# A gated recurrence with a low-rank mixer on one Trainium2 core: rows packed in 96 partitions, logarithms of the first groups summed by matmul, and a new instruction order

## The chip, the cores and the metric

The kernel runs on one core of a Trainium2 chip. The metric is the device time of one execution in microseconds (us); the time before is the median of three runs. Profiles are of one execution each. Engines in the profile are PE (TensorE matmuls), PEld (TensorE weight loads), DVE (VectorE), ACT (ScalarE), POOL (GpSimd) and SP (SyncE, which here issues nearly all DMAs).

## What is computed

The inputs are float32: q, k, v, a_re, a_im of shape (4, 8, 768, 48), that is 4 batches, 8 heads, 768 steps, 48 features, and U (768 x 32), V (32 x 768), w_ch1 (384 x 1536), w_ch2 (1536 x 384). The first half is a recurrence with a complex decay per feature, the second a mixer:

```
mag = sqrt(a_re^2 + a_im^2);  scale = min(mag, 0.999) / (mag + 1e-6)
for t in range(768):                     # per batch and head
    S = (a[t] * scale[t])[:, None] * S + outer(k[t], v[t])     # complex S, 48 x 48
    y[t] = q[t] @ real(S)
x = y as (4, 768, 384)
u = x + (x^T @ U @ V)^T
out = u + relu(u @ w_ch1) @ w_ch2
```

## The kernel before, in words

**Chunks and groups.** The sequence is cut into 24 chunks of 128 steps (6 a batch). Two chunks make a group; groups are numbered 0 to 11. The decays turn into sums of logarithms of magnitudes and sums of angles along the chunk, so that the recurrence becomes matrix products inside a chunk plus a state G (features x 48 per head) carried from chunk to chunk.

**Per group** (`gates`, lines 617 to 821). `magnitudes_of` computes on ScalarE and VectorE two arrays per step and feature: `l`, the clamped half logarithm of the squared magnitude, and `y`, the logarithm of one plus 1e-6 over the magnitude. Their sum is the logarithm that is summed along time. In the kernel before, VectorE adds them in place (group 0: a tensor_scalar and an add, lines 658 and 660; later groups: a ScalarE Relu and a fused subtract-and-add, lines 662 and 663). `within` then sums along time with matmuls against constant 0/1 matrices: `es ps` and `ef ps`, 128 x 384 each, exponentials of which scale q and k; `of_blocks` sums over blocks into `tot`, whose exponential E goes by four DMAs on SP to the transposed array T. Groups 3 to 11 (`SPLIT`) split each float32 array into two rounded halves (GS) and use the faster fp32r matmul; groups 0 to 2 use plain float32 matmuls (lines 696 and 735). A float32 matmul shows as two records in the trace.

The angle is arctan on ScalarE, times a sign of a_re (n), shifted by a quarter turn. Groups 0 to 2 (`BITS`) take the sign on VectorE from the sign bit; groups 3 to 11 take it with a ScalarE Sign (line 681) and scale and shift with a ScalarE Identity (line 763). Groups 0 to 2 add the quarter turn with one more matmul (line 799). The phase sum `ph` follows by matmul, F is its fraction of a turn, and `cs` holds cosine and sine.

**Per chunk.** `prep` multiplies q and k by es and by cs into QKC (per head a row of cosine part and a row of sine part, each 48 long in a space of 64), and transposes it on TensorE (line 860): 112 rows, of which 48 to 63 are a gap of zeros. `chain` builds products of blocks (inner, corners), scales by T on VectorE, and computes the state update dk (line 996, tile columns 0 to 63 and 64 to 111) and the output y.

**The mixer** (`mixer`) runs per two chunks once a batch is through: rank, mixed, uTp, up, down, and from m = 7 on products with fewer multiplications (few).

**The order.** Nothing is scheduled at run time. Every operation has a number in one common order of all engines, written out in `ORDER`; each engine's instructions stand in the order of these numbers. `SPARE` says before which operation how many units of filler are to be issued: matmuls of the 128 x 128 identity into a free PSUM tile (`idle`, lines 1507 to 1520), at most three units to a matmul, a unit being 128 columns. Where no PSUM tile is free, none is issued. The kernel before asks for 153 units; its program holds 91, of which 8 stand before the first es ps, 9 between it and the first ef ps. Filler waits for nothing but its PSUM tile, and later matmuls stand behind it.

Of the kernel before, what the change touches and what calls it, by code (L numbers as in the profile page):

```python
# [39 lines left out]
        ("POOL", "load"): {0: [14], 1: [34], 1.5: [84], 2: [31]},  # L40
        ("DVE", "load"): {1: [58]},
# [6 lines left out]
        ("ACT", "gates"): {0: [1, 2, 4, 6, 7, 16, 17, 22, 23, 29, 28, 45, 70, 71], 1: [24, 27, 38, 39, 41, 42, 46, 47, 65, 64, 67, 68], 2: [129, 108,  # L48
# [10 lines left out]
        ("DVE", "gates"): {0: [5, 8, 13, 18, 19, 54, 49], 1: [30, 21, 40, 43, 44, 51, 50], 2: [111, 143, 156, 185, 169], 4: [277, 322, 323, 372, 356],  # L59
# [109 lines left out]
        ("POOL", "small"): {0: [932, 933], 1: [1119, 1116, 1117], 2: [1337, 1278, 1338], 3: [1670, 1446, 1515], 4: [1778, 1776, 1777], 5: [2049, 1855,  # L169
        2008], 6: [2154, 2101, 2162], 7: [2343, 2276, 2342], 8: [2633, 2632, 2648], 9: [2629, 2634, 2663], 10: [2635, 2627, 2636]},  # L170
        ("POOL", "angles"): {6: [615], 8: [708, 733], 10: [882, 931], 12: [1097], 14: [1273, 1302], 16: [1472, 1516], 18: [1669], 20: [1879, 1913],
        22: [2039, 2077]},
        ("DVE", "mixing"): {7: [2018, 2019, 2021, 2030, 2032, 2024, 2040, 2102, 2108, 2115, 2120, 2125, 2027]},
}

# [1413 lines left out]
```

## Time and profile before

| quantity | value |
|---|---|
| runs | 626.64, 626.9, 627.37 us; median 626.9 |
| span of the profiled execution | 627.0 us; 0.1 above the median |
| busy time: PE, PEld | 609.9, 526.2 us |
| busy time: DVE, ACT, POOL | 499.7, 415.8, 38.1 us |
| PE busy in filler (line 1519) | 30.6 us |
| first es ps, first inner, first rank matmul begin | 8.79, 31.28, 116.27 us |

The span runs from the first to the last instruction of the execution. Matmuls are pipelined, so a record's duration is longer than the distance from one start to the next; distances between starts tell what a matmul costs TensorE. In a line of a timeline stand start, duration, engine, line of the kernel, operation, output and inputs, shapes, count, and in brackets the idle time of the engine before it with what ended it.

### The profile page before, as it was taken

What the parts mean: (1) busy time and instruction counts of PE and PEld (TensorE: products, weight loads), DVE (VectorE), ACT (ScalarE), POOL (GpSimd) and SP (SyncE); (2) the same over time, 40 slices, a digit from 0 to 9 for tenths busy, and PEclk for the clock granted to TensorE, in tenths of its full rate; (3) what the DMA queues carried; (4) which work ended last, traced back from release to release, by engine and by line L of the source; (5) the groups of instructions that cost most, each with busy time, mean ns of one, the idle gap of its engine ahead of it and who ended that gap; (6) DMA issues with size and microseconds to landing.
All of it is one profiled execution on the core that took longest, in us unless ns stands there. A gap on an engine that the chain in (4) does not pass through costs nothing.

```text
span 627.0 us, 23447 instructions
## 1 busy us (share of the span) xinstructions
PE 609.9 (97%) x10380; PEld 526.2 (84%) x10380; DVE 499.7 (80%) x887; ACT 415.8 (66%) x807; POOL 38.1 (6%) x79
## 2 busy tenths in 40 slices
PE   6998989999999999999999999999999999999998
PEld 3566767666889889889989989888999998999997
DVE  6899999888999979758977867788989884464554
ACT  6999999999898988687787867688433431202010
POOL 5000000000001010010000100000100100000100
PEclk7999999999999999999999999999999999999999
DMA  8864565644143252541512512601203020000101
GB/s 211 191 146 115 135 136 132 155 111 104 33 80 76 50 120 44 99 89 28 99 37 46 113 40 46 124 19 25 63 21 60 9 51 3 1 1 1 45 14 44
DMA packets 173685, 45.74 MB, mean 73 GB/s; under 512 B 167632, under 2 KB 170384, under 8 KB 173584
## 3 DMA queue, kind: packets, MB, share of 16 engines
q1 hardware_dynamic: 171376, 39.90, 30.1%
q0 software_dynamic: 2208, 4.35, 2.1%
q8 instruction: 81, 1.33, 0.9%
q14 instruction: 20, 0.16, 0.1%
HBM read 33.59 MB, written 4.72 MB: 61 GB/s over the span
## 4 chain that ended last, share of the span: by engine, by line
PE 77%; ACT 4%; DVE 3%; DMA 1%; issue 1%; SPq 0%; ACTq 0%; DVEq 0%
PE down L1356 24%; PE up L1122 15%; PE few L1222 11%; PE dk L996 3%; PE tr L860 3%; PE y L1035 3%; PE inner L910 2%; PE down L1313 2%; PE inner L907 2%; PE tot L741 2%; PE y L1027 2%; PE mixed L1089 2%; PE es ps L692 1%; PE ef ps L692 1%; PE uTp L1107 1%; PE corners L971 1%
## 5 line engine op out<-in xcount | busy, mean ns | idle before, releaser
L1122 PE MATMUL up<-uT,w 128*128 128x256 f32 x504 | 116.9, 383 | 0.0
L387 DVE TENSOR_TENSOR QK<-QK,T 112x512 f32<-112x512 f32 (+2 forms) x144 | 102.1, 732 | 8.4 <-PE inner L910 4.3
L1122 PEld LDWEIGHTS up<-uT,w 128*128 128x128 f32 x504 | 93.6, 190 | 12.5
L1356 PE MATMUL down<-w,h 128*128 128x192 f32 x396 | 72.2, 331 | 0.0
L384 ACT ACTIVATE gate<-gate 128x768 f32<-128x768 f32 (+1 forms) x82 | 64.8, 795 | 7.4 <-DVE GS L791 3.2
L1356 PEld LDWEIGHTS down<-w,h 128*128 128x128 f32 x396 | 64.1, 190 | 1.5 <-issue 0.7
L871 ACT COPY QK<-tr 112x512 f32<-112x512 f32 x96 | 51.2, 590 | 14.6 <-PE tr L860 14.3
L390 DVE TENSOR_TENSOR xo<-down,xo 128x192 f32<-128x192 f32 (+1 forms) x79 | 29.9, 387 | 27.5 <-PE down L1356 27.0
L387 DVE TENSOR_TENSOR QKC<-qk,cs 128x768 f32<-128x768 f32 x44 | 41.7, 955 | 6.3 <-ACT cs L384 3.6
L1230 ACT COPY h<-few 128x512 f32<-128x512 f32 x30 | 17.2, 586 | 40.8 <-PE few L1222 40.8
L1356 PE MATMUL down<-stage 128*128 128x192 f32 x198 | 37.6, 331 | 0.0
L1111 ACT COPY uT<-uTp 128x384 f32<-128x384 f32 x22 | 10.0, 479 | 41.4 <-PE uTp L1107 26.9
L1222 PE MATMUL few<-gate,w 128*128 128x128 f32 x280 | 34.8, 275 | 0.0
L1298 POOL DMA_DIRECT2D out_dram<-xo x32 | 19.2, 644 | 243.3 <-DVE xo L390 140.0
L860 PEld LDWEIGHTS tr<-ident,QKC 64*112 64x112 f32 x768 | 24.5, 130 | 10.7 <-issue 4.7
L1222 PEld LDWEIGHTS few<-gate,w 128*128 128x128 f32 x280 | 33.3, 192 | 0.0
L1356 PEld LDWEIGHTS down<-stage 128*128 128x128 f32 x198 | 32.1, 190 | 0.7 <-issue 0.2
L779 POOL DMA_DIRECT2D gate<-F x15 | 12.0, 799 | 327.9 <-DVE w L578 113.5
L860 PE MATMUL tr<-ident,QKC 64*112 64x64 f32 x768 | 29.4, 221 | 2.3 <-DVE QKC L387 1.6
L381 ACT ACT_TABLE_LOAD x24 | 30.8, 1283 | 1.1 <-PEq L1573 0.7
L384 ACT ACTIVATE h<-up 128x512 f32<-128x512 f32 x42 | 24.6, 596 | 9.8 <-PE up L1122 9.5
L976 ACT COPY AT<-corners 32x128 f32<-32x128 f32 x96 | 24.2, 255 | 9.6 <-PE corners L971 8.3
(200 smaller groups left out, 1285.4 us busy)
## 6 DMA issues: line engine op xcount, KB each, us to landing
stage<-in_moe_w_ch_dram SPq DMA_DIRECT2D x12, 768.0 KB, 5.0
qk<-in_q_dram SPq DMA_DIRECT2D x24, 192.0 KB, 3.2
qk<-in_k_dram SPq DMA_DIRECT2D x24, 192.0 KB, 2.7
VP<-in_v_dram SPq DMA_DIRECT2D x24, 192.0 KB, 3.6
gate<-in_a_re_dram SPq DMA_DIRECT2D x22, 192.0 KB, 3.4
gate<-in_a_im_dram SPq DMA_DIRECT2D x22, 192.0 KB, 3.4
AT<-DG SPq DMA_DIRECT2D x96, 32.0 KB, 2.3
T<-E SPq DMA_DIRECT2D x48, 48.0 KB, 2.9
```

Source lines behind the costliest of these rows:

```text
L381: ACT(1.37, rank, lambda: nc.scalar.preload_act_table_set(name), writes=[TABLE])
L384: return nc.scalar.activation(out=o, in_=i, func=f, **kw)
L387: nc.vector.tensor_tensor(out=o, in0=a, in1=b, op=OP.mult)
L390: nc.vector.tensor_tensor(out=o, in0=a, in1=b, op=OP.add)
L860: nc.tensor.transpose(out=get(*ps[r])[0:DQ, h], in_=get(*qkc)[at, h].rearrange("p u d -> p (u d)")[:, 0:DQ], identity=ident[at, at], tile_ ...
L871: nc.scalar.copy(out=to, in_=a)
L976: ACT(0.36, RR, lambda r=r, u=u: nc.scalar.copy(out=get(*ATi).rearrange("p (a u) t -> p a u t", u=2)[r:r + BLK, :, u, BLK:2 * BLK], in_=ge ...
L996: nc.tensor.matmul(out=get(*dk[r])[x:end, h], lhsT=get(*ks)[at, h, x // DP, 0:end - x], rhs=get(*VPi)[at, h], start=True, stop=True, tile_ ...
L1122: nc.tensor.matmul(out=get(*ps)[:, e], lhsT=w1[:, f, (ff + e) * 128:(ff + e + 1) * 128], rhs=get(*uT)[:, f], start=(f == 0), stop=(f == KD ...
L1222: nc.tensor.matmul(out=get(*ps)[:, q], lhsT=w()[:, q * 128:(q + 1) * 128], rhs=v[0](), start=(n == 0 and q == 0), stop=True, skip_group_ch ...
L1298: queue.dma_start(out=out[b, c * CH:(c + 1) * CH, lo:hi], in_=get("xo", i)[:, lo:hi])
L1356: nc.tensor.matmul(out=get(*to)[:, part], lhsT=x(j), rhs=y[:, j], start=(first and j == 0), stop=(j == KH - 1), skip_group_check=not first)
```

## The change

Four things are done to the arithmetic and one to the order:

1. The rows of QKC and T lie without a gap: 96 rows (cosine 0 to 47, sine 48 to 95) in place of 112. The memsets of the gap go. The transposes have 96 columns of weights in place of 112, the second tile of dk 32 in place of 48, and the VectorE and ScalarE operations on QK, T, G and GM 96 partitions in place of 112.
2. In groups 0 to 2, `y` and `l` are not added on VectorE; es ps, ef ps and tot are each accumulated by two matmuls, one on y and one on l. Groups 1 and 2 lose the ScalarE Relu for a VectorE tensor_scalar, as group 0 had it.
3. All groups take the sign from the sign bit on VectorE.
4. In groups 3 to 11 the quarter turn is added in the copy that splits z in two halves, and in the difference after it; the ScalarE Identity goes.
5. `ORDER` and `SPARE` are replaced as a whole. The new `SPARE` asks for 154 units, and the program holds all: 60 before the first es ps (20 matmuls of 384 columns in a row), then 13, 6, 20, 10, 6, 3, 7 and 4 up to the transposes of the second chunk, 25 later. On SP, the four loads of group 0's gates and the small constants go ahead of the first load of w_ch1. On TensorE, es ps and ef ps of both first chunks follow one another directly, then both tot.

The diff without `ORDER`:

```diff
-SPARE = {20: 8, 32: 9, 62: 1, 66: 1, 73: 1, 82: 5, 91: 1, 113: 6, 116: 1, 119: 8, 140: 8, 153: 6, 157: 4, 167: 1, 168: 1, 207: 6, 216: 1, 217: 1, 282:
-         1, 352: 2, 436: 1, 514: 5, 518: 5, 527: 4, 546: 4, 547: 25, 551: 12, 596: 2, 601: 1, 606: 3, 624: 1, 632: 3, 646: 1, 653: 1, 664: 1, 672: 2,
-         678: 5, 694: 1, 695: 1, 717: 1, 718: 2}
+SPARE = {23: 60, 83: 13, 90: 6, 106: 20, 127: 10, 129: 6, 131: 3, 139: 7, 144: 4, 258: 12, 442: 2, 481: 4, 608: 3, 617: 4}
...
+    DQ = 2 * D
     DP = 64
-    DQ = DP + D
...
-        QKC.append(singles.tile([128, H, 2, DP], FP, name="QKC%d" % n))
-        nc.gpsimd.memset(QKC[n][:, :, :, D:DP], 0.0)
+        QKC.append(singles.tile([128, H, 2, D], FP, name="QKC%d" % n))
...
-        nc.gpsimd.memset(TS[n], 1.0)
...
-            if on_dve:
+            if g not in SPLIT:
                 DVE(c_one(W), R1, lambda: nc.vector.tensor_scalar(out=t(l), in0=t(l), scalar1=-0.5, scalar2=-LNMAX, op0=OP.mult,
                                                                   op1=OP.max), [], [L])
-                DVE(cd, R1, lambda: add(t(l), t(l), t(y)), Y, [L])
...
-            if g in BITS:
-                DVE(c_one(W), R1, lambda: nc.vector.tensor_scalar(out=t(n).bitcast(U32), in0=t(ar).bitcast(U32), scalar1=0x80000000,
-                                                                  scalar2=INV_PI, op0=OP.bitwise_and, op1=OP.bitwise_or), AR, [N])
-            else:
-                ACT(ca + 0.09, R1, lambda: act(t(n), t(ar), AF.Sign, bias=tiny), AR, [N])
+            DVE(c_one(W), R1, lambda: nc.vector.tensor_scalar(out=t(n).bitcast(U32), in0=t(ar).bitcast(U32), scalar1=0x80000000,
+                                                              scalar2=INV_PI, op0=OP.bitwise_and, op1=OP.bitwise_or), AR, [N])
...
-                    PE(0.65, R1, lambda: nc.tensor.matmul(out=get(*to), lhsT=m.bitcast(FP), rhs=of(l, i), start=True, stop=True),
-                       [L, name], [to, ("sums", g, i)], takes=[keeps], steps=2)
+                    def two():
+                        for u, a in enumerate((y, l)):
+                            nc.tensor.matmul(out=get(*to), lhsT=m.bitcast(FP), rhs=of(a, i), start=(u == 0), stop=(u == 1))
+                    PE(1.3, R1, two, [L, y + (i,), name], [to, ("sums", g, i)], takes=[keeps], steps=4)
...
-                        nc.tensor.matmul(out=get(*ps)[u * 64:u * 64 + w, p], lhsT=get(*l)[:, h:h + w], rhs=total, start=True,
-                                         stop=True, tile_position=(0, u * 64))
+                        for n, a in enumerate((y, l)):
+                            nc.tensor.matmul(out=get(*ps)[u * 64:u * 64 + w, p], lhsT=get(*a)[:, h:h + w], rhs=total, start=(n == 0),
+                                             stop=(n == 1), tile_position=(0, u * 64))
...
-            if g not in BITS:
-                ACT(ca + 0.09, R2, lambda: act(t(z), t(z), AF.Identity, scale=1.0 / math.pi, bias=fourth), [], Z)
...
-                    ACT(c_act(DM), R2, lambda: nc.scalar.copy(out=of(a, i), in_=of(z, i)), [zi], [a + (i,)])
+                    ACT(c_act(DM) + 0.09, R2, lambda: act(of(a, i), of(z, i), AF.Identity, bias=fourth), [zi], [a + (i,)])
...
-                DVE(c_dve(DM), R2, lambda: nc.vector.tensor_tensor(out=of(b, i), in0=of(z, i), in1=of(a, i).bitcast(FP), op=OP.subtract),
-                    [zi, a + (i,)], [b + (i,)])
+                DVE(c_dve(DM), R2, lambda: nc.vector.scalar_tensor_tensor(out=of(b, i), in0=of(z, i), scalar=0.25, in1=of(a, i).bitcast(FP),
+                                                                          op0=OP.add, op1=OP.subtract), [zi, a + (i,)], [b + (i,)])
...
-                        nc.tensor.transpose(out=get(*ps[r])[0:DQ, h], in_=get(*qkc)[at, h].rearrange("p u d -> p (u d)")[:, 0:DQ],
+                        nc.tensor.transpose(out=get(*ps[r])[0:DQ, h], in_=get(*qkc)[at, h].rearrange("p u d -> p (u d)"),
...
-                        nc.tensor.matmul(out=get(*dk[r])[x:end, h], lhsT=get(*ks)[at, h, x // DP, 0:end - x], rhs=get(*VPi)[at, h],
+                        nc.tensor.matmul(out=get(*dk[r])[x:end, h], lhsT=get(*ks)[at, h].rearrange("p u d -> p (u d)")[:, x:end], rhs=get(*VPi)[at, h],
```

More of the change, by code (lines that the diff above doesn't have):

```diff
@@ L30 @@
 ORDER = {
[9 rows of a table removed]
-        ("POOL", "load"): {0: [14], 1: [34], 1.5: [84], 2: [31]},
-        ("DVE", "load"): {1: [58]},
[6 rows of a table removed]
-        ("ACT", "gates"): {0: [1, 2, 4, 6, 7, 16, 17, 22, 23, 29, 28, 45, 70, 71], 1: [24, 27, 38, 39, 41, 42, 46, 47, 65, 64, 67, 68], 2: [129, 108,
[10 rows of a table removed]
-        ("DVE", "gates"): {0: [5, 8, 13, 18, 19, 54, 49], 1: [30, 21, 40, 43, 44, 51, 50], 2: [111, 143, 156, 185, 169], 4: [277, 322, 323, 372, 356],
[10 rows of a table removed]
-        ("ACT", "angles"): {0: [72, 86, 98, 100, 103], 1: [76, 106, 112, 114, 126], 2: [210, 231, 251, 240, 241, 242, 263, 269, 271], 4: [375, 395,
[5 rows of a table removed]
@@ L172 @@
-        22: [2039, 2077]},
-        ("DVE", "mixing"): {7: [2018, 2019, 2021, 2030, 2032, 2024, 2040, 2102, 2108, 2115, 2120, 2125, 2027]},
-}
-SPARE = {20: 8, 32: 9, 62: 1, 66: 1, 73: 1, 82: 5, 91: 1, 113: 6, 116: 1, 119: 8, 140: 8, 153: 6, 157: 4, 167: 1, 168: 1, 207: 6, 216: 1, 217: 1, 282:
-         1, 352: 2, 436: 1, 514: 5, 518: 5, 527: 4, 546: 4, 547: 25, 551: 12, 596: 2, 601: 1, 606: 3, 624: 1, 632: 3, 646: 1, 653: 1, 664: 1, 672: 2,
-         678: 5, 694: 1, 695: 1, 717: 1, 718: 2}
[9 rows of a table added]
+        ('POOL', 'load'): {0: [22], 1: [55], 1.5: [594], 2: [41]},
@@ new lines @@
+        ('DVE', 'load'): {1: [18]},
[6 rows of a table added]
+        ('ACT', 'gates'): {0: [0, 4, 2, 9, 14, 10, 16, 43, 51, 32, 36, 44, 61, 64], 1: [6, 12, 24, 29, 25, 31, 40, 45, 49, 47, 53, 59], 2: [122, 89,
[10 rows of a table added]
+        ('DVE', 'gates'): {0: [8, 27, 28, 15, 62, 58], 1: [13, 21, 30, 34, 50, 73], 2: [113, 155, 149, 192, 200], 4: [236, 310, 306, 327, 336], 6:
[10 rows of a table added]
+        ('ACT', 'angles'): {0: [68, 84, 95, 92, 101], 1: [71, 97, 105, 107, 116], 2: [197, 228, 247, 238, 240, 242, 266, 268, 286], 4: [374, 397, 415,
[5 rows of a table added]
+        ('DVE', 'angles'): {0: [77, 85], 1: [78, 98], 2: [210, 232, 248], 4: [378, 401, 416], 6: [577, 590, 592, 600, 614, 615, 630], 8: [688, 705,
[4 rows of a table added]
@@ new lines @@
+        ('DVE', 'prep'): {0: [93, 102, 104], 1: [119, 125, 137], 2: [204, 244, 251], 3: [277, 288, 295], 4: [390, 422, 433], 5: [392, 439, 471], 6:
[6 rows of a table added]
+        ('ACT', 'prep'): {0: [112, 108, 118, 120], 1: [145, 147, 151, 152], 2: [260, 259, 264, 263], 3: [308, 313, 339, 340], 4: [443, 441, 445, 444],
[4 rows of a table added]
+        ('DVE', 'rest'): {0: [117, 154, 159, 193, 142, 162, 183], 1: [178, 227, 231, 261, 213, 234, 237, 256], 2: [269, 315, 326, 357, 293, 323, 328,
[8 rows of a table added]
+        ('DVE', 'levels'): {0: [121, 134, 140, 132, 135, 143], 1: [168, 207, 212, 187, 201, 217], 2: [270, 281, 292, 279, 287, 311], 3: [352, 364,
[9 rows of a table added]
@@ new lines @@
+        ('ACT', 'levels'): {0: [138], 1: [208], 2: [300], 3: [391], 4: [470], 5: [519], 6: [751], 7: [837], 8: [946], 9: [1008], 10: [1156], 11:
[14 rows of a table added]
+        ('ACT', 'rest'): {0: [177, 186, 179, 171, 221, 215, 220], 1: [252, 254, 250, 253, 280, 282, 273], 2: [356, 355, 359, 353, 377, 379, 381], 3:
[10 rows of a table added]
+        ('ACT', 'small'): {0: [596, 290, 362, 504, 383, 483, 612, 566, 611, 628], 1: [726, 752, 803, 811, 777, 823, 858], 2: [958, 893, 1094, 1131,
[4 rows of a table added]
+        ('DVE', 'small'): {0: [276, 606, 618, 627, 636, 665, 673, 664, 645, 652, 732, 743], 1: [687, 734, 686, 821, 844, 854, 861, 872, 882, 904, 915,
[25 rows of a table added]
@@ new lines @@
+        ('POOL', 'small'): {0: [801, 750], 1: [1099, 947, 1069], 2: [1334, 1264, 1425], 3: [1614, 1507, 1535], 4: [1749, 1702, 1777], 5: [2031, 1930,
+        1953], 6: [2216, 2142, 2206], 7: [2377, 2223, 2364], 8: [2637, 2634, 2636], 9: [2524, 2541, 2618], 10: [2606, 2621, 2639]},
+        ('POOL', 'angles'): {6: [603], 8: [703, 736], 10: [878, 892], 12: [1080], 14: [1270, 1294], 16: [1457, 1479], 18: [1628], 20: [1840, 1884],
+        22: [2007, 2081]},
+        ('DVE', 'mixing'): {7: [1997, 2010, 2001, 2011, 2029, 2000, 2039, 2092, 2102, 2120, 2113, 2114, 2056]},
+}
@@ L301 @@
     PL = H * HC
-    BITS = range(SPLIT[0])
     PUT = (0, 2), (4, 6), (8, 10)
@@ L443, in w2_of @@
         return w2.rearrange("p (j x) m -> p j x m", x=2)[:, :, x, y * DH:(y + 1) * DH]
-    leps, lmax, tiny = column("leps", math.log(1e-6)), column("lmax", LNMAX), column("tiny", 1e-30)
+    leps, lmax = column("leps", math.log(1e-6)), column("lmax", LNMAX)
     magic, fourth, quarter = column("magic", MAGIC), column("fourth", 0.25), column("quarter", math.pi / 2)
@@ L744, in of_blocks @@
             else:
-                PE(0.51, R1, sums, [l, ("total", 0), ("sums", g)], [ps], way=1, takes=[e], steps=4 * HH)
+                PE(0.82, R1, sums, [l, y + (i,), ("total", 0), ("sums", g)], [ps], way=1, takes=[e], steps=8 * HH)
             used = 2 * D if g in SPLIT else 64 + D
@@ L988, in chain @@
         for r in parts_k:
-            psum(dk[r], "Y", [128, H, D], [128, H, DP])
+            psum(dk[r], "Y", [128, H, D], [128, H, HC])
         def state(h0):
```

23 lines of the change are left out of this document (6 added, 17 removed), and 248 rows, old and new, of the table ORDER.

## The prediction

> **What bounds the kernel now.** I read the page's busy shares first, then the table of busy times by stretch for TensorE alone, cut at the places that matter here, then the timeline of TensorE up to the first row sums.
>
> ```profile
> PE 609.9 (97%) x10380; PEld 526.2 (84%) x10380; DVE 499.7 (80%) x887; ACT 415.8 (66%) x807; POOL 38.1 (6%) x79
> ```
>
> TensorE is busy for 609.9 of 627.0 us, so its own timeline can be used as a ledger: the span is its work, plus its fillers (the matmuls of `ident` that `idle` issues), plus its waits.
>
> ```profile
> core 0: us, PE busy (x), PEclk, DMA share, GB/s
> 0.00:1.42 1.42, 0.00 (x0) 1.00 0.00 0
> 1.42:5.00 3.58, 3.58 (x6) 1.00 0.87 164
> 5.00:8.79 3.79, 0.01 (x1) 0.91 0.94 272
> 8.79:14.92 6.13, 6.12 (x10) 0.50 1.02 260
> 14.92:31.28 16.36, 14.82 (x167) 1.00 0.82 187
> 31.28:116.27 84.99, 79.36 (x2019) 1.00 0.58 135
> 116.27:157.00 40.73, 39.43 (x365) 1.00 0.49 117
> 157.00:600.00 443.00, 442.61 (x7664) 1.00 0.25 50
> 600.00:627.00 27.00, 23.97 (x169) 1.00 0.10 34
> ```
>
> The second column is the length of the stretch, the third TensorE's busy time. Its waits are 1.42 us before `ident` exists, 3.03 us at the end (the last sum and its store), and between them 3.79 + 1.54 + 5.63 + 1.30 + 0.39 = 12.65 us. All but 0.39 us of these lie before 157 us; from there to 600 us TensorE alone sets the pace, and nothing that VectorE or ScalarE saves there is worth time. Before that, another engine is full too:
>
> ```profile
> 48.00:64.00 16.00, 14.16 (x412) 10.81 (x411) 15.86 (x25) 15.36 (x32) 0.00 (x0) 1.00 0.47 107
> 64.00:80.00 16.00, 15.30 (x385) 11.29 (x384) 16.00 (x28) 15.79 (x31) 0.00 (x0) 1.00 0.59 142
> 80.00:96.00 16.00, 13.85 (x399) 10.39 (x398) 15.97 (x25) 15.75 (x32) 0.00 (x0) 1.00 0.57 136
> ```
>
> Here the columns are TensorE, its weight loads, VectorE, ScalarE and GpSimd. VectorE (15.97 of 16) and ScalarE are full, and TensorE waits for them. So a change decides the time in two ways: by what it adds to or takes from TensorE anywhere, and by when the chain of the first groups lets VectorE begin.
>
> **The fillers and the first matmuls.** This part weighs most, and it is in the new order, not in the arithmetic.
>
> ```profile
> 1.42 3.58 PE L1519 MATMUL tr<-ident 128*128 128x384 f32 x6 [1.42 <-POOL ident masks.py:199]
> 8.79 1.62 PE L696 MATMUL es ps<-GL,mid 128*128 128x384 f32 x2 [3.79 <-DVE GL L390]
> 10.21 4.05 PE L1519 MATMUL tr<-ident 128*128 128x384 f32 x6
> 13.42 0.56 DVE L390 TENSOR_TENSOR GL<-GL,gate 128x384 f32<-128x384 f32 x1
> 14.05 1.25 PE L696 MATMUL ef ps<-GL,fore 128*128 128x384 f32 x2
> 15.13 0.39 PE L1519 MATMUL tr<-ident 128*128 128x128 f32 x2
> 15.35 0.81 PE L696 MATMUL es ps<-GL,mid 128*128 128x384 f32 x2
> 16.00 0.81 PE L696 MATMUL ef ps<-GL,fore 128*128 128x384 f32 x2
> 16.64 0.39 PE L1519 MATMUL tr<-ident 128*128 128x128 f32 x2
> 17.69 1.09 PE L735 MATMUL tot<-total,GL 128*64 128x32 f32 x32 [0.66 <-ACT es L384]
> 21.59 0.91 PE L801 MATMUL ph<-gate,prefix 128*128 128x384 f32 x2
> 26.23 0.27 PE L860 MATMUL tr<-ident,QKC 64*112 64x64 f32 x1 [0.23 <-DVE QKC L387]
> 31.28 0.89 PE L910 MATMUL inner<-QK 112*32 112x48 f32 x64
> ```
>
> A float32 matmul leaves two records. Nine units of filler (one unit is 128 columns) run from 10.21 to 14.05: 0.427 us each. At full clock a matmul of 384 columns starts 0.65 us after the one before (15.35 to 16.00): 0.215 us a unit. The granted clock was 0.50 in 8.79:14.92 and 1.00 after it, so TensorE ran 6.13 us on end before it sped up, and the 3.58 us at the start, at the same slow pace, hadn't sufficed.
>
> The kernel before issues 91 units: 8, then 9 at the slow pace (3.58 + 3.84 = 7.4 us), then 74 spread out. The order of the changed program has 154: **60 in one block before the first es ps**, then 13, 6, 20, 10, 6, 3, 7, 4 up to the second chunk's transposes, and 25 later. They wait for nothing, and what stands behind them waits for all of them. I take the slow pace for 6.13 us again: 14.4 units by 7.55, the other 45.6 x 0.215 = 9.8, and the first es ps starts at 17.3 us where it started at 8.79. It is ready earlier: both chunks' logarithms were done at 13.98 (the row at 13.42), behind more loads than the new order puts ahead of them. The block costs 15.9 for 7.4: **+8.5 us**. Bounds: full clock from 5.00 on gives a start at 16.1 (-1.2), one more microsecond or two at half pace +1.3. The Trainium skill (TensorE: Matmul & The Clock Gate, section "What's actually happening") lets the clock rise after one busy window of about 3.4 us that runs freely; by 3.4 us the start would be near 15.8 and the sum 1.5 us less, and here the first stretch of 3.58 us speaks against the short end.
>
> ScalarE feels the block at once: in its new order the two exponentials of es stand ahead of the x logarithm and reciprocal of both chunks, so arctan, F, cs and QKC are queued behind the block. Following the new order of TensorE behind 17.3: eight matmuls 5.2, 32 tot 2.2, four ph and one carry 3.3, 55 units 11.8, 32 transposes 1.1, 16 dk 0.6: the first inner at 41.5, against 31.28. Waits cover none of it, for the other engines' steps are shorter than TensorE's: from the end of tot (18.78) to ph of z (21.59) they took 2.8, and TensorE now has two ph and 13 units there, 4.1; from there to the transposes (26.23) 4.6, against 7.5 now; from there to the inner 5.1, against 5.1. On SP both chunks' gates go ahead of the first weight load, and on GpSimd five memsets go; both only make operands earlier that the block then holds back.
>
> The other 94 units against 74: 20 x 0.215 = **+4.3 us**.
>
> **Logarithms summed on TensorE.** In the first three groups es ps, ef ps and tot take y and l one after the other. That is 12 matmuls of 384 columns more, 12 x 0.65 = 7.8, and 48 of tot at 1.09 / 16 = 0.068 each, 3.3. Against it, one es ps and one ef ps were at half pace (10.21 - 8.79 = 1.42, 15.13 - 14.05 = 1.08) and aren't any more: -1.2. **+9.9 us** (11.1 at 0.75 a matmul, as after a short tile).
>
> **Packing in 96.** No moving operand gets shorter; only weight loads do: the transposes' from 112 to 96 columns, the second tile of dk from 48 to 32.
>
> ```profile
> 66.03 1.16 PE L860 MATMUL tr<-ident,QKC 64*112 64x64 f32 x32
> 67.12 2.86 PE L1122 MATMUL up<-uT,w 128*128 128x256 f32 x12
> 43.17 1.12 PE L735 MATMUL tot<-total,w 128*64 128x32 f32 x32
> 44.22 1.56 PE L1519 MATMUL up<-ident 128*128 128x384 f32 x4
> 104.73 1.47 PE L741 MATMUL tot<-total,GL 128*96 128x32 f32 x16
> 106.03 0.60 PE L692 MATMUL ef ps<-GS,fore 128*128 128x384 f32 x2
> L860 PEld LDWEIGHTS tr<-ident,QKC 64*112 64x112 f32 x768 | 24.5, 130 | 10.7 <-issue 4.7
> ```
>
> Thirty-two transposes take 1.09 us, 68 ns a pair of halves. What a column of weights costs I estimate from tot: 96 columns 1.30 / 16 = 81 ns, 64 with 48 beside them 1.05 / 16 = 66 ns: 0.47 ns a column. 16 x 0.47 = 7.5 ns for each of 384 pairs: **-2.9 us**; bounds 0, if the load is hidden, and -5.8, if both of a pair count. In dk the tile beside stays at 64 columns: 0, at most -2.4. VectorE and ScalarE go by elements per partition, so 96 for 112 gives them nothing.
>
> **Signs, quarter turn, adds.**
>
> ```profile
> L384 ACT ACTIVATE gate<-gate,tiny 128x768 f32<-128x768 f32 x9 | 8.4, 938 | 0.0
> L384 ACT ACTIVATE gate<-gate,fourth 128x768 f32<-128x768 f32 x9 | 8.4, 931 | 2.3 <-DVE gate L760 2.1
> L384 ACT ACTIVATE GL<-GL,lmax 128x768 f32<-128x768 f32 x10 | 9.3, 930 | 0.1
> L578 DVE TENSOR_SCALAR w<-w 128x768 uint32<-128x768 uint32 x12 | 6.7, 562 | 0.0
> L390 DVE TENSOR_TENSOR GL<-GL,gate 128x384 f32<-128x384 f32 x2 | 1.1, 568 | 0.3 <-ACT gate L384 0.2
> ```
>
> ScalarE loses 9 signs, 9 quarter turns and one Relu in each of groups 1 and 2: 8.4 + 8.4 + 1.9 = 18.7 us. VectorE gains 9 x 0.56 = 5.0 and loses two adds (1.1) and about 0.4 in each of groups 1 and 2. Nearly all of it falls behind 100 us. I cost it at nothing: TensorE's work hides it, and if that cover were gone, the 5.0 would be the most it could cost. Before 116 us it helps only through waits, which come next.
>
> **Waits.** With TensorE later and fuller before 116 us, the 3.79 is filled, and much of 1.54 + 5.63 + 1.30 goes: VectorE's operations between the first inner and the rank matmuls stay about as many, TensorE's grow from 72.5 without fillers and waits to about 80, plus 32 units in either order. I leave 3.5 of 12.65: **-9.1 us**. Bounds: all gone (-12.65), or only the first gone (-3.8). Thirty-one runs of fillers become fourteen, and a run costs about 0.1 us beside its units when the tile shape changes: **-1.7** (0 to -3.4).
>
> **Sum**, against the profiled execution: 627.0 + 8.5 + 4.3 + 9.9 - 2.9 - 9.1 - 1.7 = **636.0 us**. Its span of 627.0 stands 0.1 above the median of 626.9, which changes nothing.
>
> **The rivals.**
> (1) VectorE holds the early stretch. Its 15.97 of 16 speaks for it: starting 10 us later it can't catch up, and all waits but the first stay. TensorE's larger work and the shorter chain of each group speak against it. 636.0 + (8.9 - 3.5) = 641.4; with a microsecond or two of new waits 643.
> (2) Weight loads bind. Each of the 768 transposes and 704 second tiles of dk gives its 16 columns: 1472 x 16 x 0.47 = 11.1 in place of 2.9, so 627.8, the same time. Speaking against it: a load lasts 130 ns and transposes start every 34 ns, so loads overlap. The Trainium skill (same page, section "LDWEIGHTS (loading the stationary operand)") gives columns / 1.2 GHz, so 13 ns for 16 columns, and 768 transposes would give 10.2 us; the 34 ns show that this can't all be on the path.
> (3) **Faster**: TensorE's early instructions are off the path. Then fillers and added matmuls only stand where it waited, VectorE and ScalarE, shorter by some 2 us before 116, set the stretch, and fewer fillers (11 units, 2.4) and waits (1.3) come after it: about 621. It holds if the first es ps isn't late; the sum turns at a start near 8.3 us, for which 60 units would have to run in 6.9 us, 0.115 each, half of what the row shows.
> (4) The packing does nothing: 636.0 + 2.9 = 638.9, within the forecast.
>
> **How the numbers follow.** Forecast (631 to 640, with case 4) 0.62; VectorE holds it 0.20; weight loads bind 0.12; faster 0.06. The low bounds together (-1.2, -3.5, -2.9, -2.4, -1.7) would give 624, the high ones 646; neither is likely whole. 628 to 643 leaves out the faster case and the ends of the first two rivals, under 2 in 10. Differences of 0.2% (1.25 us) are about what a measurement of this kernel can tell from none. Faster 0.07 (case 3 and the edge of case 2), same 0.09, slower 0.84.
>
> **What would show it.** The first es ps at 16 to 17.6 us with TensorE busy from 1.42 on; the first inner near 41 and the first rank matmul (116.27 now) near 130; waits between start and end of 2 to 6 us; 32 transposes in 1.0 us; ScalarE's busy time near 398, VectorE's near 503. Wrong would be: a first es ps before 10 us; a rank matmul before 120, which would mean the fillers fell into slack; or transposes at half their time.

## The result, and the profile after

The changed kernel takes **869.7 us** (median of 4 runs, 866.7 to 874.0) against 627.1 us (626.6 to 628.0) for the kernel before in the same comparison: 1.385 times as long, 95% interval 1.380 to 1.391. The prediction was 636.0 us with a range of 628 to 643. It had the sign right and the size wrong by 234 us. The profiled execution has a span of 868.2 us.

From the page of the changed kernel: the span, the busy shares, the granted clock in 40 slices, the chain of work by line, and the costliest of all groups.

```profile
span 868.2 us, 23718 instructions
PE 849.4 (98%) x10520; PEld 690.5 (80%) x10520; DVE 502.8 (58%) x893; ACT 402.6 (46%) x787; POOL 35.7 (4%) x74
...
PEclk9997697799798877898977977978966987989999
...
PE dk L989 22%; PE down L1349 18%; PE up L1115 12%; PE few L1215 8%; PE tr L1512 3%; PE tr L853 3%; PE y L1028 3%; PE inner L903 2%; PE down L1306 2%; PE inner L900 1%; PE y L1020 1%; PE up L1512 1%; PE tot L735 1%; PE mixed L1082 1%; PE uTp L1100 1%
...
L989 PE MATMUL dk<-VP,QKC 64*64 64x48 f32 (+1 forms) x1408 | 196.1, 262 | 0.9 <-ACT xo L1039 0.8
```

The same group on the page of the kernel before:

```profile
L996 PE MATMUL dk<-VP,QKC 64*64 64x48 f32 (+1 forms) x1408 | 27.9, 217 | 0.5 <-DVE QKC L387 0.3
```

TensorE still waits for almost nothing: 868.2 - 849.4 = 18.8 us, as before (627.0 - 609.9 = 17.1). VectorE and ScalarE have busy times close to the predicted ones (502.8 and 402.6; the prediction said 503 and 398). Nearly all the added time is in what TensorE shows as busy. The state update `dk`, the same 1408 records as before, went from 27.9 to **196.1 us**: 168 of the 241 us that the span grew. And the granted clock, 1.00 nearly all through before, is mostly 0.6 to 0.9.

The timeline of TensorE shows a call of dk (16 matmuls, or 32 where two calls stand back to back) at full clock (39.92), one in which the clock falls (68.94, mean 0.70) and one at half clock (91.36, 0.50), each with the line that follows it, so that starts can be subtracted.

```profile
1.42 16.22 PE L1512 MATMUL tr<-ident 128*128 128x384 f32 x40 [1.42 <-POOL ident masks.py:199]
17.48 0.81 PE L689 MATMUL es ps<-gate,mid 128*128 128x384 f32 x2
...
39.92 3.60 PE L989 MATMUL dk<-VP,QKC 64*64 64x48 f32 x32
43.44 1.56 PE L1512 MATMUL up<-ident 128*128 128x384 f32 x4
44.93 0.89 PE L903 MATMUL inner<-QK 96*32 96x48 f32 x64
...
68.94 8.93 PE L989 MATMUL dk<-VP,QKC 64*64 64x48 f32 x64
77.80 1.65 PE L794 MATMUL ph<-w,prefix 128*128 128x384 f32 x2
...
91.36 10.74 PE L989 MATMUL dk<-VP,QKC 64*64 64x48 f32 x64
102.03 5.10 PE L1115 MATMUL up<-uT,w 128*128 128x256 f32 x12
```

Thirty-two records take 43.44 - 39.92 = 3.52 us: 110 ns a record, 0.22 us a matmul of two records. The two later calls of 64 take 8.86 us (138 ns a record) and 10.67 us (167 ns). In the kernel before, 64 take 1.07 us:

```profile
50.32 1.14 PE L996 MATMUL dk<-VP,QKC 64*64 64x48 f32 x64
51.39 0.91 PE L799 MATMUL ph<-fourth,prefix 128*128 128x384 f32 x2
```

The table by stretch of the changed kernel (length; PE, weight loads, VectorE, ScalarE and GpSimd busy; granted clock; DMA share; GB/s):

```profile
64.00:80.00 16.00, 15.43 (x168) 9.94 (x160) 8.53 (x16) 7.53 (x13) 0.00 (x0) 0.76 0.45 107
80.00:96.00 16.00, 14.96 (x236) 10.21 (x234) 11.28 (x17) 12.05 (x24) 0.00 (x0) 0.71 0.17 32
96.00:112.00 16.00, 16.00 (x146) 12.05 (x145) 5.66 (x9) 4.08 (x6) 0.00 (x0) 0.67 0.26 72
```

TensorE is busy for 15 to 16 of 16 us at a granted clock of 0.67 to 0.76, with 146 to 236 records where the kernel before had 385 to 412 in its stretches of the same length. VectorE, which was full there, is now busy for 5.7 to 11.3 us.

### The profile page after: what moved, and what is told of

Its sections match the earlier page's. It is cut to its first block, busy times and chain, and to the rows that moved or that the text cites. A ratio compares the mean times of both kernels' runs of the same rounds, so it can differ in the third digit from the quotient of the medians.

```text
span 868.2 us, 23718 instructions
## 1 busy us (share of the span) xinstructions
PE 849.4 (98%) x10520; PEld 690.5 (80%) x10520; DVE 502.8 (58%) x893; ACT 402.6 (46%) x787; POOL 35.7 (4%) x74
## 4 chain that ended last, share of the span: by engine, by line
PE 89%; issue 5%; ACT 3%; DVE 2%; DMA 1%; SPq 0%; POOL 0%; ACTq 0%; POOLq 0%
PE dk L989 22%; PE down L1349 18%; PE up L1115 12%; PE few L1215 8%; PE tr L1512 3%; PE tr L853 3%; PE y L1028 3%; PE inner L903 2%; PE down L1306 2%; PE inner L900 1%; PE y L1020 1%; PE up L1512 1%; PE tot L735 1%; PE mixed L1082 1%; PE uTp L1100 1%
## 5 line engine op out<-in xcount | busy, mean ns | idle before, releaser
L989 PE MATMUL dk<-VP,QKC 64*64 64x48 f32 (+1 forms) x1408 | 196.1, 262 | 0.9 <-ACT xo L1039 0.8
L989 PEld LDWEIGHTS dk<-VP,QKC 64*64 64x64 f32 (+1 forms) x1408 | 136.7, 142 | 59.4 <-ACT xo L1039 0.9
L1115 PE MATMUL up<-uT,w 128*128 128x256 f32 x504 | 134.7, 427 | 0.0
L1115 PEld LDWEIGHTS up<-uT,w 128*128 128x128 f32 x504 | 107.3, 217 | 18.0
L384 DVE TENSOR_TENSOR QK<-QK,T 96x512 f32<-96x512 f32 (+2 forms) x144 | 102.2, 726 | 22.6 <-PE inner L903 14.2
L864 ACT COPY QK<-tr 96x512 f32<-96x512 f32 x96 | 51.1, 585 | 98.5 <-PE tr L853 98.3
L1349 PE MATMUL down<-w,h 128*128 128x192 f32 x396 | 82.2, 359 | 0.0
L381 ACT ACTIVATE F<-ph,magic 128x384 f32<-128x384 f32 x24 | 13.9, 579 | 80.8 <-PE ph L789 67.3
L387 DVE TENSOR_TENSOR GM<-GM,dk 96x384 f32<-96x384 f32 x20 | 10.9, 547 | 57.6 <-PE dk L989 57.5
L915 DVE COPY_PREDICATED DG<-mask,inner 128x128 f32<-128x128 int32 (+1 forms) x72 | 24.4, 340 | 17.0 <-PE inner L900 14.0
```

Of the source, the lines that this page charges most:

```text
L381: return nc.scalar.activation(out=o, in_=i, func=f, **kw)
L384: nc.vector.tensor_tensor(out=o, in0=a, in1=b, op=OP.mult)
L387: nc.vector.tensor_tensor(out=o, in0=a, in1=b, op=OP.add)
L864: nc.scalar.copy(out=to, in_=a)
L915: nc.vector.copy_predicated(out=to, mask=part(mask[:, n], "p").unsqueeze(1).to_broadcast(list(to.shape)), data=a if t == BLK else a.rearra ...
L989: nc.tensor.matmul(out=get(*dk[r])[x:end, h], lhsT=get(*ks)[at, h].rearrange("p u d -> p (u d)")[:, x:end], rhs=get(*VPi)[at, h], start=Tr ...
```

## The experiments

**Theory.** The code of dk changed by one number: its second tile is 32 columns wide where it was 48. A call alternates the two tiles (first 64 columns, then the rest) at every matmul. If a tile of 48 columns counts as one of 64, the width never changed in the kernel before, and it changes at every matmul of dk now. The theory is that TensorE must empty itself at each such change, at about 0.18 us, and that the array, empty half the time, is then granted less clock, which slows everything else. Rivals: a tile of 32 columns is slow by itself, whatever stands beside it; weights read at a stride of 96 in place of 64 are slow to load; or the new order is at fault. The Trainium skill (TensorEngine Tiling (Array Packing), section "Key Properties") states the first half: "Changing tiling mode (not just tile) drains the TensorE"; it gives no price. The runs below agree with it and give one for this case, though no run shows the drain itself.

Five runs change dk in the changed kernel, five put parts of the change into the kernel before, four take parts of the new order back. The kernel before took 628.4 to 629.7 us beside them. Each computes the whole result.

### Five ways to write dk

**The second tile 48 wide again** (`a_dk48`): rows stay packed in 96, but the tile's weights reach 16 columns on, into the next head's row; the 16 rows of the result that this adds are read by nobody. The tile QKC gets 16 spare columns at its end.

```diff
-                    for x, end in ((0, DP), (DP, DQ)):
-                        nc.tensor.matmul(out=get(*dk[r])[x:end, h], lhsT=get(*ks)[at, h].rearrange("p u d -> p (u d)")[:, x:end], ...
+                    for x, w in ((0, DP), (DP, D)):
+                        a = get(*ks)[at, h].rearrange("p u d -> p (u d)")[:, x:x + 32]
+                        nc.tensor.matmul(out=get(*dk[r])[x:x + w, h], lhsT=bass.AP(tensor=a.tensor, offset=a.offset, ap=[a.ap[0], [1, w]]), ...
```

> The changed kernel with one thing undone: dk's second tile loads 48 weight columns again (the last 16 belong to the next head and land in PSUM rows that nobody reads), so both tiles of dk are 64 x 64; the packing in 96 stays. Theory A (dk now alternates between tiles of 64 and of 32 columns, and each change empties the array, after which the clock gate halves the clock): dk falls from 196 to about 28 us busy, the granted clock is 1.00 behind the start, and the time is 632 to 642, by the fillers and added matmuls of the prediction. Theory B (weights read at a stride of 96 in place of 64 are slow to load): dk stays near 196 and the time near 870.

Measured: 659.2 us (657.6 to 666.0), ratio 1.051 (1.048 to 1.055), span 655.9, mean granted clock 0.995 where the changed kernel had 0.874. The group of dk, and its first call in the timeline:

```profile
L992 PE MATMUL dk<-VP,QKC 64*64 64x48 f32 (+1 forms) x1408 | 27.8, 217 | 1.2 <-ACT xo L1042 0.8 <-DVE QKC L384 0.3
```

```profile
35.28 1.10 PE L855 MATMUL tr<-ident,QKC 64*96 64x64 f32 x32
36.31 2.42 PE L1515 MATMUL up<-ident 128*128 128x384 f32 x8
38.66 0.68 PE L992 MATMUL dk<-VP,QKC 64*64 64x48 f32 x32
39.26 1.56 PE L1515 MATMUL up<-ident 128*128 128x384 f32 x4
40.75 0.89 PE L905 MATMUL inner<-QK 96*32 96x48 f32 x64
...
71.64 0.67 PE L1031 MATMUL y<-G,QK 96*64 96x48 f32 x14 [1.04 <-ACT xo L1042]
...
135.45 2.14 PE L1066 MATMUL rank<-xo,UV 128*32 128x384 f32 x24
```

Sixteen weight columns *more* in every second matmul, at the same stride of 96, and 210 us go: the stride falls as a rival. The first call takes 39.26 - 38.66 = 0.60 us for its 32 records instead of 3.52. With 16 matmuls in the call, (3.52 - 0.60) / 16 = **0.18 us** for each change of width, at full clock. The theory holds for dk; the 659 is 17 us above what I expected of this kernel, which the last group of runs takes up.

**One matmul of 96 columns** (`a_dk96`), per head and half, no second tile:

```diff
-                    for x, end in ((0, DP), (DP, DQ)):
-                        nc.tensor.matmul(out=get(*dk[r])[x:end, h], ... tile_position=(r * HC, x))
+                    nc.tensor.matmul(out=get(*dk[r])[0:DQ, h], ... tile_position=(r * HC, 0))
```

> The changed kernel with dk as one matmul of 96 weight columns per head and half in place of two tiles; packing and order stay. Theory A: no two widths within dk, so no emptying: 704 records of 96 columns, at about 35 to 75 ns each 25 to 50 us busy, clock 1.00, time 632 to 660. Theory B: the stride is the same, dk stays far above 100 us and the time above 780.

Measured: 670.8 us, ratio 1.068 (1.064 to 1.072), clock 0.979, dk 41.1 us in half as many records. Without a change of width inside a call most of the cost is gone, but one wide tile takes longer than two narrow ones side by side.

**Three tiles of 32** (`a_dk32x3`):

```diff
-                    for x, end in ((0, DP), (DP, DQ)):
+                    for x, end in ((0, 32), (32, 64), (64, DQ)):
```

> The changed kernel with dk in three tiles of 32 columns each (0, 32, 64), so one width and 1056 matmuls in place of 704. Theory A: no change of width; 2112 records at 12 to 20 ns, 25 to 42 us busy, time 635 to 655. Theory C: three slow tiles for one, dk near 400 us or more and the time over 1000.

Measured in a single run: 666.7 us, span 664.9.

```profile
L989 PE MATMUL dk<-VP,QKC 64*32 64x48 f32 x2112 | 26.9, 210 | 5.2 <-issue 4.9 <-DVE QKC L384 0.3
```

Half as many matmuls again, all of them 32 wide, and dk takes 26.9 us, less than in the kernel before. A tile of 32 isn't slow. That rival falls.

**Sorted by width.** Two kernels issue the very matmuls of the changed one in another sequence. `a_sorted`: in each call all tiles of 64, then all tiles of 32, two changes a call. `a_headsort`: in each head two of 64, then two of 32, which is half the changes.

```diff
 a_sorted
+            for x, end in ((0, DP), (DP, DQ)):
                 for h in range(h0, h0 + HH):
                     for r in parts_k:
...
-                    for x, end in ((0, DP), (DP, DQ)):
 a_headsort
             for h in range(h0, h0 + HH):
+                for x, end in ((0, DP), (DP, DQ)):
                     for r in parts_k:
...
-                    for x, end in ((0, DP), (DP, DQ)):
```

> The changed kernel with the same matmuls of dk in another order: within each call all tiles of 64 columns first, then all of 32. Theory A: two changes of width for each call of 4 heads, under 100 in all in place of some 700; dk 30 to 60 us busy, time 635 to 670. Theory C (a tile of 32 columns at column 64 is slow in itself, some 0.4 us each): dk stays near 196 and the time near 870.

> The changed kernel with dk's matmuls in another order: for each head the two tiles of 64 columns (both halves), then the two of 32, so 16 changes of width for each chunk of 32 matmuls in place of 32. If each change of width costs a fixed time (0.22 - 0.04 = 0.18 us at full clock), the time of dk lies half way between 28 and 196 us, 100 to 120 (less if the clock stays up: 28 + 352 x 0.18 = 91), and the span at 740 to 780. If instead the 32-column tile as such is slow unless all of them stand together, dk stays above 170. The kernel sorted by calls, with 4 changes a chunk, had 53.

Measured, a single run each: 683.7 us (span 681.9, clock 0.990) and 743.5 us (span 741.8, clock 0.954).

```profile
L989 PE MATMUL dk<-VP,QKC 64*64 64x48 f32 (+1 forms) x1408 | 53.2, 216 | 0.3 <-DVE QKC L384 0.3
```

```profile
L989 PE MATMUL dk<-VP,QKC 64*32 64x48 f32 (+1 forms) x1408 | 94.0, 233 | 1.1 <-ACT xo L1039 0.8 <-DVE QKC L384 0.3
```

The same instructions, the same operands, the same tiles: dk takes 196.1, 94.0 or 53.2 us (27.8 without changes) as the widths change 704, about 384 or 96 times. Over 27.8 that is 0.24, 0.17 and 0.26 us a change. So it is the change that costs. Why the three quotients differ can be read from the starts of single records in the traces. At full clock, the record behind a change starts 0.14 us after the one before it in all three (means 0.141, 0.141 and 0.143 us); in `a_dk48`, records of 64 and 48 columns follow each other at 0.014. At half clock it is 0.22, and in the changed kernel 325 of the 679 changes between records of dk fall there. The rest of the loss lies between the changes, for the sequence also changes which tiles stand side by side: in the first call of `a_sorted` the matmuls of 64 columns start 58 ns apart and those of 32 columns 43 ns, against 38 ns for the four tiles in turn in `a_dk48`. So the 0.26 of the sorted kernel is mostly not the price of a change.

The times, other than dk, came out above the expectations for all four of `a_dk48`, `a_dk96`, `a_dk32x3` and `a_sorted`, by 11 to 17 us over the upper ends: I had taken the new order at its forecast price.

### Parts of the change in the kernel before

**The packing alone**, in the old order with the old arithmetic: once with the second tile of 32 as in the change (`b_pack`), once with 48 (`b_pack48`).

```diff
-    DQ = DP + D
+    DQ = 2 * D
...
-        QKC.append(singles.tile([128, H, 2, DP], FP, name="QKC%d" % n))
+        QKC.append(singles.tile([128, H, 2, D], FP, name="QKC%d" % n))
...
-                        nc.tensor.matmul(out=get(*dk[r])[x:end, h], lhsT=get(*ks)[at, h, x // DP, 0:end - x], ...
+                        nc.tensor.matmul(out=get(*dk[r])[x:end, h], lhsT=get(*ks)[at, h].rearrange("p u d -> p (u d)")[:, x:end], ...
```

> The kernel before, in its own order, with only the packing in 96, as the change has it (dk's tiles 64 and 32 columns wide). Theory A: this alone carries most of the loss; dk 160 to 210 us busy, mean granted clock 0.85 to 0.93, time 780 to 860. Rival (the slow dk needs the new order around it, such as calls of dk split apart): below 700.

> The kernel before, in its own order, with only the packing in 96, and dk's second tile loading 48 columns so that both tiles are 64 x 64. Theory A: no emptying; the transposes load 96 columns for 112, which took 1.03 us for 32 in the runs so far against 1.09: 24 x 0.06 = 1.4 us less, 624 to 628, dk near 28 us, clock as before. Rival (the packing itself costs, by its stride or its places in T): above 632.

Measured: `b_pack` 844.2 us, ratio 1.332 (1.325 to 1.339), span 841.3, clock 0.866. `b_pack48` 628.4 us against 629.2, ratio 0.9987 (0.9975 to 0.9998). The dk group and the clock of `b_pack`, and the transposes of `b_pack48`:

```profile
PEclk9797867999898877979968977978977977899999
...
L994 PE MATMUL dk<-VP,QKC 64*64 64x48 f32 (+1 forms) x1408 | 192.7, 259 | 0.6 <-DVE QKC L387 0.3 <-ACT xo L1044 0.2
```

```profile
64.99 1.16 PE L860 MATMUL tr<-ident,QKC 64*96 64x64 f32 x32
66.07 2.86 PE L1123 MATMUL up<-uT,w 128*128 128x256 f32 x12
```

One part, by itself, in the order of the kernel before, gives 215 us of the loss. The order isn't to blame for it. This run also shows the clock falling while TensorE is busy. Its first call of dk runs from 29.16 to 37.56 us (same columns as the table by stretch above):

```profile
29.16:33.00 3.84, 3.84 (x37) 2.84 (x36) 1.99 (x4) 3.78 (x5) 0.00 (x0) 1.00 0.87 162
33.00:34.00 1.00, 1.00 (x9) 0.72 (x10) 0.00 (x0) 0.19 (x1) 0.00 (x0) 0.77 0.86 276
34.00:37.56 3.56, 3.56 (x23) 2.40 (x22) 0.00 (x0) 0.00 (x0) 0.00 (x0) 0.50 0.29 121
37.56:42.71 5.15, 5.15 (x71) 3.17 (x70) 3.36 (x5) 2.82 (x4) 0.00 (x0) 0.50 0.01 3
```

TensorE shows no wait, and the granted clock goes from 1.00 to 0.50 inside the call and stays there for the matmuls behind it. `b_pack48`, in the same order, keeps 1.00 from 26 to 44 us. And the packing with a tile of 48 is worth 0.8 us, barely outside the uncertainty and less than the 1.4 expected: 32 transposes take 1.08 us instead of 1.09. This is the only version whose interval lies below 1, and its gain is less than the 0.2% that I called no difference.

**Signs and quarter turn** (`b_arith`): `b_pack48` with parts 3 and 4 of the change. The numbers of the ScalarE instructions that go are dropped from the order, the new VectorE ones stand in their place.

> The kernel before, in its own order, with the packing (second tile of dk at 48 columns), the sign from the bits in all groups, and the quarter turn in the split copy; 9 signs and 9 quarter turns leave ScalarE, 9 bit operations join VectorE at the numbers of the signs. Logarithms, order of the rest and fillers stay. If the arithmetic is worth little because TensorE sets the pace, 623 to 627, within 1 us of the packing alone; if ScalarE's 17 us were worth something in the stretch from 116 to 157, 618 to 623; slower than 629 if the bit operation delays VectorE.

Measured: 629.0 us against 629.2, ratio 0.9996 (0.9984 to 1.0007). ScalarE's busy time falls from 415.8 to 403.7 us and VectorE's grows from 499.7 to 503.1, for nothing; 623 to 627 was expected.

**Logarithms on TensorE** (`b_logs`): part 2 alone; the second matmul of each sum stands directly behind the first.

> The kernel before, in its own order and with its fillers, with only the logarithms of groups 0 to 2 summed on TensorE: 12 matmuls of 384 columns and 48 of tot more, two adds and two Relus fewer. By the prediction's step 9.9 to 11.1 us of work on TensorE; if none of it falls into waits, 636 to 640; if the early waits (3.8 before the first es ps, 7.2 up to the rank matmuls) take most of it, 627 to 632.

Measured: 637.3 us against 628.4, ratio 1.014 (1.012 to 1.016): +8.9 us. The first rank matmul begins at 125.86 (before: 116.27), so the loss is there by then.

**The filler block** (`b_fill60`): the kernel before with 60 units ahead of the first es ps instead of 8.

```diff
-SPARE = {20: 8, 32: 9, ...
+SPARE = {20: 60, 32: 9, ...
```

> The kernel before with 60 units of filler ahead of the first es ps in place of 8, nothing else. By the prediction's step the block is carried whole: the first es ps at 16 to 17.6 in place of 8.79, and 5 to 8 us more in all, since some waits shrink: 632 to 636. Rival (the block falls into slack that the early stretch has): 626 to 629.

Measured: 637.8 us against 629.2, ratio 1.014 (1.011 to 1.016): +8.6 us. Its timeline:

```profile
1.43 15.10 PE L1519 MATMUL tr<-ident 128*128 128x384 f32 x40 [1.43 <-POOL ident masks.py:199]
16.36 0.81 PE L696 MATMUL es ps<-GL,mid 128*128 128x384 f32 x2
```

The first es ps comes 7.6 us later than in the kernel before, and nothing later makes up for it: the loss is a little above the 5 to 8 us expected.

### What the new order costs without the width changes

`a_dk48` is 30 us slower than the kernel before, so the forecast would have been wrong without the width changes too. The largest entry among TensorE's waits is one that the kernel before lacks: y waiting for ScalarE.

```profile
PE y L1031 <- ACT xo L1042: 6.7, 13, 1.7
```

(total, times, longest). The 13 ScalarE copies of y stand in the new order between two halves of the same chunk's y matmuls. `a_dk48_xo` moves those 13 numbers behind the last y matmul of their chunk; `a_dk48_fill8` cuts the block from 60 units to 8; `a_dk48_both` does both; `a_dk48_both_add` then lets VectorE add the logarithms of groups 0 to 2 again (part 2 of the change undone).

```diff
 a_dk48_fill8, a_dk48_both, a_dk48_both_add
-SPARE = {23: 60, 83: 13, ...
+SPARE = {23: 8, 83: 13, ...
 a_dk48_both_add
+                DVE(cd, R1, lambda: add(t(l), t(l), t(y)), Y, [L])
...
-                        for u, a in enumerate((y, l)):
-                            nc.tensor.matmul(out=get(*to), lhsT=m.bitcast(FP), rhs=of(a, i), start=(u == 0), stop=(u == 1))
+                    nc.tensor.matmul(out=get(*to), lhsT=m.bitcast(FP), rhs=of(l, i), start=True, stop=True)
```

> The changed kernel with dk's second tile at 48 columns, and 8 units of filler ahead of the first es ps in place of 60. If the block is carried whole in this order too: first es ps near 9 to 11, 6 to 9 us less than the 659 of the kernel with the second tile at 48. Rival (other fillers and VectorE hold the stretch, so the start is made up later): within 2 us of it.

> The changed kernel with dk's second tile at 48 columns, and 13 ScalarE copies of y into xo moved in the order from between the y matmuls of a chunk to behind them. TensorE waited 6.7 us in 13 places for these copies, in the middle of the products with the state; the kernel before has none there. Theory: waits gone, 5 to 8 us less than the 659 with the second tile at 48. Rival (TensorE then waits elsewhere, for PSUM or for VectorE): within 2 us of it.

> The changed kernel with dk's second tile at 48 columns, 8 units of filler at the start in place of 60, and the 13 copies behind the y matmuls. If both count in full: 643 to 648. What is left above the kernel before is then the logarithms on TensorE (about 10) and the other places of the new order.

> The changed kernel with dk's second tile at 48 columns, 8 units at the start, the 13 copies behind the y matmuls, and the logarithms of groups 0 to 2 added by VectorE again, one matmul each on the sum. In the order of before, the sums on TensorE cost 8.9 us. If they cost the same here, 644 falls to 634 to 636, and some 6 us are the rest of the new order; if the new order had hidden them, 640 to 645, and some 14 us are the order.

| kernel | us | ratio to the kernel before | first rank matmul |
|---|---|---|---|
| a_dk48 | 659.2 | 1.051 (1.048 to 1.055) | 135.45 |
| a_dk48_fill8 | 652.6 | 1.039 (1.037 to 1.041) | |
| a_dk48_xo | 650.0 | 1.034 (1.032 to 1.036) | |
| a_dk48_both | 644.1 | 1.024 (1.022 to 1.026) | 126.81 |
| a_dk48_both_add | 646.5 | 1.028 (1.025 to 1.031) | |

The block is worth 6.6 us in this order, the place of the copies 9.2, both together 15.2. The copies also explain why TensorE was busy longer in y: 50.5 us in `a_dk48`, 45.9 in the kernel before, 45.7 in `a_dk48_xo` (sums over the three groups of y).

The last run is a miss. In the old order the adds on VectorE are worth 8.9 us; given back here, they bring nothing (646.5 against 644.1; the intervals of the two ratios overlap). Two stretches of that run (length, PE busy, clock, DMA share, GB/s) show where it went in the profiled execution, which with 650.2 us was the slowest of five:

```profile
64.00:80.00 16.00, 13.03 (x281) 0.99 0.40 93
80.00:96.00 16.00, 15.82 (x270) 0.58 0.66 148
```

In `a_dk48_both` TensorE is busy for 15.31 and 15.05 us there, at a clock of 1.00. With fewer matmuls TensorE stands still for 3 us in the first stretch and gets little more than half clock in the second; the first rank matmul comes at 133.63, later than with the added matmuls. So in this order they seem to cover waits in part; one profile doesn't prove it. Some 15 us of the new order, against the kernel before, are left in `a_dk48_both`: 10.5 us lie ahead of the first rank matmul (126.81 against 116.27) and the others behind it. Which places they are at wasn't separated and **stays open**.

## Why the prediction was wrong

**The step that failed** is "Packing in 96", at its last term: "In dk the tile beside stays at 64 columns: 0, at most -2.4." I looked at the width of the weights and asked what is saved by loading 16 columns fewer. I didn't ask what the narrower tile does to its neighbour. It measured +168 us in dk itself. The sentence that should have stopped me stands in the prediction itself: I costed a run of fillers at about 0.1 us beside its units "when the tile shape changes", and dk changes its tile's shape at each of 704 matmuls. At that price alone it would have been 70 us, far above every other term. `b_pack` shows the step by itself: the packing, forecast at -2.9 us, cost 215. The rule of the Trainium skill speaks for it in so many words (TensorEngine Tiling (Array Packing), "Key Properties"), and I weighed other pages and not this one.

**And its second half**: nothing in my sum let the clock fall while TensorE is busy. Between `a_dk48` and the changed kernel PE's busy time grows by 849.4 - 636.5 = 212.9 us; 168.3 of it is dk and 44.6 is in matmuls that are the same in both. The up group, for example:

```profile
L1115 PE MATMUL up<-uT,w 128*128 128x256 f32 x504 | 134.7, 427 | 0.0
```

```profile
L1118 PE MATMUL up<-uT,w 128*128 128x256 f32 x504 | 117.8, 387 | 0.1
```

16.9 us more (first the changed kernel, then `a_dk48`); the down groups together gain 17.4. Among `a_dk48`, the two sorted kernels and the changed one the clock falls with the changes of width: 0.995, 0.990, 0.954, 0.874 for none, 96, 384 and 704, and `b_pack` shows it falling inside a call of dk. Changes of width aren't the only way down, though: `a_dk96` has none inside its calls and 0.979. That the clock falls *because* the array stands empty inside records that show as busy is argued; no run shows the array's inside. The Trainium skill (TensorE: Matmul & The Clock Gate, "What's actually happening") has half clock come back after an idle window of about 3.4 us. The changed kernel's trace shows no wait of that length (the longest between matmuls is 2.46 us), so the rule fits only if time inside busy records counts as idle.

**Rivals.** (1) and (4) lay within 628 to 643 and (2), at 627.8, just below, so none could hold the result; (3) is ruled out by the first es ps at 17.48. Nor does (1) hold in `a_dk48`: VectorE is busy there for 14.50 and 14.30 us of 64 to 80 and 80 to 96, not for all 16. Rival (2) asked about the narrower second tiles of dk, the right instructions, and only for their gain.

**The waits, -9.1 us: wrong.** I left 3.5 us between start and end. `a_dk48` has 655.9 - 636.5 = 19.4 in all, 8.0 by my forecast: 11.4 too few. Neither the y waits (6.7 us) nor their effect on y's busy time (+4.6) was in the sum. I read the new order only as far as the first inner and took it to be as well matched afterwards as the old one, whose TensorE is busy for 99.8% of 200 to 400 us. `a_dk48` isn't (length, PE busy, clock, DMA share, GB/s):

```profile
200.00:300.00 100.00, 97.48 (x1994) 0.98 0.38 74
300.00:400.00 100.00, 98.34 (x1718) 1.00 0.32 61
```

**The transposes, -2.9: mis-sized.** Thirty-two take 36.31 - 35.28 = 1.03 us in `a_dk48` and 1.08 in `b_pack48`, from 1.09; the whole packing gave -0.8. Weight loads of transposes are nearly hidden, as the lower bound had it. The price of 0.47 ns a column came from a misreading: a float32 matmul leaves two records, so the 16 records of 96 columns are 8 matmuls at 163 ns, while the 66 ns are of a whole matmul of 64 or 48. Two of those, 131 ns, do the work of one of 96; this compares one wide tile with two narrow ones and says nothing of a column. Two sums are slightly off as well and change nothing: 3.4 us of half pace gives a start at 16.0, not 15.8, and the high bounds together 648, not 646.

**Right in mechanism and size.** The filler block: +8.5 forecast, +8.6 in `b_fill60` (which keeps the next nine units) and 6.6 in the new order (`a_dk48_fill8`); the first es ps at 16 to 17.6 forecast, 17.48 measured, with TensorE busy from 1.42 on; it fell into no slack. Logarithms on TensorE: +9.9 forecast, +8.9 in `b_logs`, though taking them out of the new order brought nothing. Signs, quarter turn: nothing forecast, nothing in `b_arith`. The first inner: 41.5 forecast, 40.75 in `a_dk48` (44.93 in the changed kernel, whose first es ps came 1.3 us later and whose first dk costs 2.9 us more). The first rank matmul was not right: 130 forecast, 135.45 in `a_dk48`. **Not tested**: the -1.7 for fewer runs of fillers, and the 4.3 for 20 more units by themselves.

So `a_dk48` exceeds the 636.0 of the sum, span against span, by 19.9 us: 11.4 in waits, 4.6 in y, 2.1 in the packing, and 1.8 that I can't place among fillers and sums.

## What to carry to other kernels

When an edit makes a tile of TensorE narrower, compare its width with that of the matmuls issued right before and after it, and count the changes: here each cost about 0.2 us, five times the 0.04 us of the matmul itself. If two widths are needed, widen the narrow tile with unread columns (dk 27.8 us here) or, second best, sort the matmuls by width (53.2). Look at the granted clock as well as at the busy time: TensorE showed 98% busy here at a mean clock of 0.874. And take a change made of several parts apart first: here the packing alone, put into the old order, showed 215 of the 243 us in a single run.

## What the runs showed of the hardware

- Not every difference in width is a change: 48 weight columns beside 64 cost nothing (dk 27.8 us in `a_dk48`), 32 beside 64 do (196.1 us), and three of 32 don't (26.9 us).
- The price of a change at full clock: 0.18 us from the first call of the changed kernel (3.52 against 0.60 us), 0.15 from that of `a_headsort`, whose 32 records take 1.82 us for 8 changes (at the change itself, one record starts 0.14 us after the other):

```profile
38.46 1.89 PE L989 MATMUL dk<-VP,QKC 64*64 64x48 f32 x32
40.28 1.56 PE L1512 MATMUL up<-ident 128*128 128x384 f32 x4
```

- Two narrow tiles side by side beat one wide one for this state update: 64 and 48 columns in two matmuls take 27.8 us in all, 96 columns in one (`a_dk96`) 41.1 us.
- How long TensorE stays at half pace after its start varies between executions that begin alike. The 60 units would take 12.9 us at 0.215 us each; they took 16.06 in the changed kernel (1.42 to 17.48), 14.93 in `b_fill60` (1.43 to 16.36) and 14.45 in `a_dk96` (1.42 to 15.87). At 0.427 us a unit in the slow part, that is 6.4, 4.1 and 3.1 us of half pace; the prediction took 6.13.
